# GpSimd pieces beside a two-instruction VectorE step: the wait is set on the instruction ahead of the step

## The chip, the cores and the metric

The kernel runs on one core of a Trainium2 chip. The core has a matrix engine (TensorE, PE in the profile, with its weight loads as PEld), a vector engine (VectorE, DVE), a scalar engine for activation functions (ScalarE, ACT), a general engine (GpSimd, POOL) and a queue engine that issues transfers (SyncE, SP). The engines run their own instruction streams in order and wait for one another on semaphores. The metric is the device time of one execution in microseconds (us); the median of the runs is compared.

## The reference

One transformer block on 2048 rows of 512 numbers, in bfloat16: a layer norm modulated by a vector `c`, self-attention with 32 heads of width 16, a gated residual, a second modulated layer norm, a two-layer network with GELU (512 to 1376 to 512) and a gated residual.

```python
mod = (_silu(c) @ w_mod).reshape(c.shape[0], 6, 1, -1)
sa, ca, ga, sb, cb, gb = (mod[:, i] for i in range(6))
h = _layernorm(x) * (1 + ca) + sa
x = x + ga * attention(h, wqkv, wo)          # 32 heads, Dh = 16, softmax over 2048 keys
h = _layernorm(x) * (1 + cb) + sb
x = x + gb * (gelu(h @ w1 + b1) @ w2 + b2)
```

The attention has 32 x 2048 x 2048 exponentials. They make up most of the work outside the matrix engine.

## The kernel before

The 2048 queries are cut into four blocks of 512. A run is one block with four heads (or, in the last block, half a block with eight), against 16 tiles of 128 keys. TensorE multiplies four heads at a time in four row groups of its array (L864) and writes scores to PSUM. Most scores go to ScalarE, which takes two or three 512-column banks in one exponential (L937, tile `st` to `pt`). The rest go to VectorE, which makes exponentials out of integer arithmetic: an L978 moves 512 scores from PSUM (tile `ax`) to a 16-bit tile `ph`, and when four of them are there, four shifted copies are made. Three or four copies are one VectorE instruction each over all 2048 numbers (L998, the shift, tile `sh`); in many tiles the last copy is made by GpSimd instead, in four pieces of 512 numbers (L1014, tile `sg`). TensorE multiplies all of them with the values (L1049, tile `od`).

Between the runs lies the rest of the block, in small portions: the normalisation of finished heads (GpSimd L1101), the scaling of weights by gates (GpSimd L1124, L1209), and for a finished block its tail. The tail has the output projection and its residual (VectorE L1282), the second layer norm, the two matrix products of the network (TensorE L1238 and L1298, VectorE L1303) and GELU (ScalarE L1308 or L1313). A layer norm takes the statistics of each 128 rows in one VectorE step of two instructions: `bn_stats` (L646, into tile `ln_s`) and `bn_aggr` (L647, into `mv`). GpSimd turns them into a reciprocal root with two small instructions (L651 and L653, tile `rs`), and VectorE applies it (L657, tile `z`).

The order of all instructions is worked out while the program is built, by a planner (class `Plan`). It keeps a clock for every engine, gives each step an estimated cost and a priority, and writes the instructions out in the order in which the steps start on its clocks. Its function `commit` puts one step on its engine and calls the step's function, which emits the instructions. Seeds (`SEEDS`, one for each 16 us) vary the planner's priorities. The engines then run in that fixed order; semaphores alone decide when each instruction starts.

GpSimd pieces are of the kind "beside": the planner places one at the start of a VectorE step that does not use the port which it takes to be shared by the two engines (`port=True` marks the steps that use it: L998 and L657 among those of VectorE). So that the chip keeps to that, each piece gets one added wait by `after_dve`: it looks back through the last 400 instructions emitted, finds the VectorE instructions among them, and waits for the last but one. The last one is taken to be the step beside which the piece is to run. Pieces with this wait are those of L1014, L1101, L1124, L1190, L1209 and L1245.

Of the kernel before, what the change touches and what calls it, by code (L numbers as in the profile page):

```python
# [13 lines left out]
ENG = mybir.EngineType  # L14
# [49 lines left out]
FILL = 2.1  # L64
# [4 lines left out]


class Res:


    def __init__(self, name, n, alloc):
        self.name, self.alloc = name, alloc
        self.free = [0.0] * n
# [34 lines left out]
class Plan:  # L111
    SLACK = {"NIL": 0.0, "PE": 0.10, "DVE": 0.05, "ACT": 0.15, "POOL": 0.05, "SP": 0.05}

    def __init__(self, dyn, later):
        self.later, self.fill_at, self.cool, self.heat, self.until = later, 0.0, 0.0, None, 1e9
        self.free = {e: 0.0 for e in self.SLACK}
        self.lists = {e: [] for e in self.SLACK}
        self.mode, self.tiles, self.now = None, {}, 0.0
        self.bus = {"SP": 0.0, "ACT": 0.0}
        self.port = {"DVE": 0.0, "POOL": 0.0}  # L120
        self.dve = (0.0, 0.0, True)
        self.dyn, self.done, self.fill = dyn, deque(), FILL

    def add(self, op):
        if op.todo == 0:
# [90 lines left out]
    def commit(self, s, o):  # L216
        self.lists[o.eng].remove(o)
        self.now = s
        if o.acq is not None:
            o.slot = min(range(len(o.acq.free)), key=lambda i: o.acq.free[i])  # L220
            o.acq.free[o.slot] = 1e18
            o.tile = o.acq.alloc(o.slot)
        if o.kind == "pv" and s >= self.cool and o.last_left() > 1:
            o.extra, o.us = True, 2 * o.us
        if o.rows is not None:
            o.row = min(o.rows, key=lambda i: self.tiles.get(i, 0.0) if self.mode == "qk" else i)
            o.mode = ("qk", o.row)
        if o.eng == "PE":
            self.done.append((s, (o.us if o.mode[0] != "qk" else o.us * (len(o.mode) - 1) / 4) * o.use))
            while self.done[0][0] < s - 30.0:  # L230
                self.done.popleft()
            tot = 0.0
            self.fill_at = self.cool = 0.0
            for t, us in reversed(self.done):
                tot += us
                if tot >= HEAT and not self.cool:
                    self.cool = t + WIN
                if tot >= self.fill:
                    self.fill_at = t + WIN
                    break  # L240
            if o.mode[0] != self.mode:
                self.mode, self.tiles = o.mode[0], {}
            for i in o.mode[1:]:
                self.tiles[i] = s + o.us
            self.free["PE"] = s + 0.01
        else:
            self.free[o.eng] = s + o.us
            if o.port:
                self.port[o.eng] = s + o.us
            if o.eng == "DVE" and o.us > 0:  # L250
                self.dve = (s, s + o.us, o.port)
        o.end = s + o.us + o.lat
        if o.kb:
            q = "SP"
            self.bus[q] = max(self.bus[q], s + o.us + 0.75) + o.kb / (300.0 if s < 12.0 else 260.0)
            o.end = self.bus[q] + 0.7
        if o.fn is not None:
            o.fn(o)
        for owner in o.rel:
            owner.uses -= 1  # L260
            owner.last = max(getattr(owner, "last", 0.0), o.end + (DVE_PE if o.eng == "DVE" else 0.0))
            if owner.uses == 0:
                owner.acq.free[owner.slot] = owner.last
        for w in o.waiters:
            w.todo -= 1
            w.ready = max(w.ready, o.end + (PV_LATE if o.eng in ("DVE", "POOL", "ACT") and w.kind == "pv" else 0.0))
            if w.todo == 0:
                self.lists[w.eng].append(w)
# [21 lines left out]
def kernel(  # L290
# [14 lines left out]
    nc = tc.nc  # L305
# [115 lines left out]
    plan = Plan(dyn, later)  # L421
# [402 lines left out]
    own = [[kt for kt in range(NT) if kt not in shared[r]] for r in range(NR)]  # L824
# [182 lines left out]
    def by_pool(r, kt, j, first, es, parts):  # L1007
        sh = op("NIL", None, 0.0, es[:1], lat=0.0, prio=0.0, acq=r_sg)
        got = []
        for h in range(4):  # L1010
            def go(o, e=es[h]):
                g_left[0] -= 1
                c = slice(e.qk.row * QB, (e.qk.row + 1) * QB)
                after_dve(nc.gpsimd.tensor_scalar(  # L1014
                    out=sh.tile[:, c], in0=first.tile[:, c], scalar1=1.0 / FINE, scalar2=PH_0 + PH_SH[j],
                    op0=ALU.mult, op1=ALU.add))
            g_left[0] += 1
            got.append(op("POOL", go, G_US, (sh, es[h]), lat=0.1, prio=G_PRIO, kind="beside", rel=(first,), port=True,
                          gate=lambda: plan.beside(G_MIN)))
        pv_op(r, kt, j, got, parts(sh), (sh,))  # L1020
# [111 lines left out]
    def beside(fn, deps, rel=(), prio=0.5, free=False, us=POOL_US):  # L1132

        if free:
            return [op("POOL", lambda o, c=c: fn(slice(c * HB, (c + 1) * HB)), us, deps, lat=0.1, prio=0.1,
                       rel=rel, port=True) for c in range(2)]
        return [op("POOL", lambda o, c=c: after_dve(fn(slice(c * HB, (c + 1) * HB))), us, deps, lat=0.1,
                   prio=prio, kind="beside", rel=rel, port=True, gate=lambda: plan.beside(POOL_MIN))
                for c in range(2)]

    def after_dve(pool):

        own = [i for i in islice(reversed(nc.cur_bb.bb.instructions), 400) if i.engine == ENG.DVE]
        if len(own) > 1:
            tc.add_manual_dep(pool.ins, own[1].name, mybir.DependencyInfo(
                mybir.DependencyClass.Sync, mybir.DependencyReason.DATA), reason="beside")


    o_late = {}

    def late_loads(after):
# [42 lines left out]
    def fold_w1():  # L1194
        sb = op("DVE", lambda o: nc.vector.tensor_copy(out=sb_bf, in_=modB[:, 0:NC]), 0.1, (o_late["mB"],), prio=1.0)

        def column(ps, f):
            for j in range(NC):
                nc.tensor.matmul(out=ps[:, f:f + 1], lhsT=W1[:, j, f * P:(f + 1) * P], rhs=sb_bf[:, j:j + 1],
                                 start=(j == 0), stop=(j == NC - 1))  # L1200
        mm = chain([(lambda ps, f=f: column(ps, f), 0.15) for f in range(NF)], [sb, o_late["w1"]], "gate", r_ax, use=0.05,
                   gate=lambda: plan.cool > plan.now + 0.0)
        o_late["b1"] = op("DVE", lambda o: nc.vector.tensor_tensor(out=b1c, in0=mm.tile[:, 0:NF], in1=b1_bf, op=ALU.add),
                          0.15, (mm, o_late["small"]), prio=1.0, rel=(mm,))
        got = []
        for j in range(NC):
            for lo in range(0, NF * P, QB):
                c = slice(lo, min(lo + QB, NF * P))
                got.append(op("POOL", lambda o, j=j, c=c: after_dve(nc.gpsimd.tensor_scalar(  # L1209
                    out=W1[:, j, c], in0=W1[:, j, c], scalar1=modB[:, NC + j:NC + j + 1], scalar2=0.0,  # L1210
                    op0=ALU.mult, op1=ALU.add)), G_US, (mm, o_late["mB"]), lat=0.1, prio=2.0, kind="beside", port=True,
                    gate=lambda: plan.beside(G_MIN)))
        o_late["w1"] = op("NIL", None, 0.0, got, lat=0.0, prio=0.0)
# [353 lines left out]
```

## Time and profile before

| | |
|---|---|
| median of three runs | 767.43 us (767.27 to 767.84) |
| the profiled execution | 767.62 us |
| its span, first to last instruction | 765.1 us |
| PE busy | 729.2 us, 95% of the span |
| DVE busy | 723.3 us, 95%, 1250 instructions |
| ACT busy | 741.3 us, 97%, 670 instructions |
| POOL busy | 329.3 us, 43%, 603 instructions |
| granted TensorE clock, mean | 0.999 |

A row of a timeline has the start in us from the beginning of the span, the duration in us, the engine, the line in the kernel, the operation, the tile written and the tile read, their shapes, and the count of instructions merged into the row. The bracket at its end is the time for which the engine sat idle before it, and what ended that. A row of a group of instructions has, after the bar, the busy time in us, the mean duration in ns, the idle time before them and who ended it. VectorE rows overlap a little: an instruction is shown to start some 0.08 us before the one ahead has ended. Busy time contains the time in which an instruction that has started is held up.

### The profile page before, as it was taken

To read this page: it belongs to the slowest core of one execution; us is meant where nothing else is said; L and a number is where in the kernel's file an instruction comes from. 1 tells how busy PE (TensorE), PEld (TensorE's weight loads), DVE (VectorE), ACT (ScalarE), POOL (GpSimd) and SP (SyncE) were. 2 spreads that over 40 slices of the span, in tenths; PEclk is the share of its full clock that TensorE was granted. 3 is DMA by queue.
4 is the path that set the end of the run, shared out by engine and by line. 5 is a ranking of instruction groups with operands and counts; after the bars stand their busy time and mean duration, and the time that the engine had idled before them with its cause. 6 is when DMAs were issued, how large, how long until landed. Compare 5 with 4: busy or idle time off the path is not lost. (4 is left out here: it accounts for less than half of the span.)

```text
span 765.1 us, 20651 instructions
## 1 busy us (share of the span) xinstructions
PE 729.2 (95%) x8142; PEld 263.4 (34%) x8142; DVE 723.3 (95%) x1250; ACT 741.3 (97%) x670; POOL 329.3 (43%) x603
## 2 busy tenths in 40 slices
PE   8999999999999999999999999999999899999998
PEld 4423333333322222222322222222233334434454
DVE  7899879999999999999999999999999999999994
ACT  4999999999999999999999999999999999999993
POOL 7513554454444444555455253342434424353421
PEclk9999999999999999999999999999999999999999
DMA  7160010010200001001101010001020102001100
GB/s 221 38 193 26 19 51 18 21 29 12 69 22 25 18 23 47 19 16 40 45 22 42 16 45 18 22 20 33 24 70 22 32 18 60 19 5 46 33 18 28
DMA packets 42162, 29.53 MB, mean 39 GB/s; under 512 B 25525, under 2 KB 35286, under 8 KB 42066
## 3 DMA queue, kind: packets, MB, share of 16 engines
q1 hardware_dynamic: 41530, 27.17, 12.9%
q8 instruction: 63, 1.03, 0.6%
q10 hardware_dynamic: 536, 1.05, 0.4%
q14 instruction: 33, 0.27, 0.1%
HBM read 20.77 MB, written 2.61 MB: 31 GB/s over the span
## 5 line engine op out<-in xcount | busy, mean ns | idle before, releaser
L937 ACT ACTIVATE pt<-st 128x1536 bf16<-128x1536 f32 x618 | 700.8, 1329 | 2.0 <-PE st L864 0.9
L978 DVE TENSOR_SCALAR ph<-ax 128x512 int16<-128x512 f32 x504 | 328.5, 680 | 13.7 <-PE ax L864 12.2
L1014 POOL TENSOR_SCALAR sg<-ph 128x512 int16<-128x512 int16 x316 | 196.4, 622 | 241.9 <-DVE sh L998 168.9
L998 DVE TENSOR_SCALAR sh<-ph 128x2048 int16<-128x2048 int16 x425 | 287.1, 708 | 1.1 <-PE od L1049 0.5
L864 PE MATMUL st<-qm,kT 32*128 32x512 bf16 x1544 | 241.8, 382 | 20.2 <-ACT pt L937 15.4
L864 PE MATMUL ax<-qm,kT 32*128 32x512 bf16 x504 | 174.4, 379 | 4.6 <-DVE ph L978 3.4
L864 PEld LDWEIGHTS <-kT 32*128 32x128 bf16 x2048 | 81.2, 91 | 237.8 <-issue 229.6
L1049 PE MATMUL od<-pt,VEB 128*32 128x512 bf16 (+1 forms) x1924 | 142.6, 341 | 0.2
L1049 PE MATMUL od<-sh,VX 128*32 128x512 bf16 (+1 forms) x1508 | 110.6, 340 | 1.2 <-DVE sh L998 0.6
L1049 PEld LDWEIGHTS <-VEB 128*32 128x32 bf16 x2560 | 61.6, 96 | 80.1 <-issue 65.7
L1049 PEld LDWEIGHTS <-VX 128*32 128x32 bf16 x1908 | 46.0, 95 | 71.7 <-issue 63.0
L1101 POOL TENSOR_TENSOR OT<-OD,RB 128x256 bf16<-128x256 f32 x38 | 28.0, 741 | 59.9 <-DVE sh L998 53.0
L1049 PE MATMUL od<-sh,VEB 128*32 128x512 bf16 (+1 forms) x636 | 49.9, 340 | 0.6 <-DVE sh L998 0.6
L489 PE MATMUL od<-warm 128*32 128x512 bf16 x472 | 45.6, 381 | 0.0
L1298 PE MATMUL ax<-blk,W 128*128 128x512 bf16 (+1 forms) x176 | 43.5, 355 | 0.8 <-DVE ph L978 0.8
L741 PE MATMUL ax<-blk,w 128*128 128x512 bf16 x124 | 35.1, 382 | 1.0 <-DVE ph L978 0.4
L1238 PE MATMUL ax<-w,g 128*128 128x512 bf16 x128 | 34.6, 381 | 1.3 <-DVE ph L978 0.8
L1101 POOL TENSOR_TENSOR OS<-OD,RB 128x256 bf16<-128x256 f32 x24 | 17.3, 728 | 40.8 <-DVE sh L998 30.0
L799 POOL TENSOR_SCALAR VX<-VEB 128x128 bf16<-128x128 bf16 x60 | 20.1, 337 | 31.2 <-DVE VEB L672 27.8
L1049 PE MATMUL od<-sg,VX 128*32 128x512 bf16 (+1 forms) x400 | 32.2, 340 | 0.1
L1303 DVE TENSOR_SCALAR g<-ax,b1c 128x512 bf16<-128x512 f32 (+1 forms) x44 | 29.1, 672 | 0.1
L646 DVE BATCH_NORM_STATS2 ln_s<-xb 128x6 f32<-128x512 bf16 x32 | 21.7, 677 | 1.6 <-DMA xb<-in_A_x_dram 1.4
(107 smaller groups left out, 410.2 us busy)
## 6 DMA issues: line engine op xcount, KB each, us to landing
RB<-rn SPq DMA_DIRECT2D x124, 64.0 KB
xb<-in_A_x_dram SPq DMA_DIRECT2D x7, 512.0 KB
out_dram<-o SPq DMA_DIRECT2D x16, 128.0 KB
qm<-qs SPq DMA_DIRECT2D x120, 16.0 KB
W<-in_B_w_dram SPq DMA_DIRECT2D x1, 1376.0 KB
w<-in_A_wqkv_dram SPq DMA_DIRECT2D x3, 384.0 KB
g<-in_w_mod_dram ACTq DMA_DIRECT2D x1, 1024.0 KB
g<-in_w_mod_dram SPq DMA_DIRECT2D x1, 1024.0 KB
```

What stands on the lines that cost most here:

```text
L489: nc.tensor.matmul(out=o_od[r].tile[32 * i:32 * i + 32, :], lhsT=warm[:, 0:32], rhs=warm[:, 0:1].to_broadcast([P, QB]), start=False, stop= ...
L741: return chain([(lambda ps, j=j: nc.tensor.matmul(out=ps[:, 0:QB], lhsT=w.tile[:, j, cc * P:(cc + 1) * P], rhs=o_h[b].tile[:, j, :], start ...
L864: nc.tensor.matmul(out=o.tile[:, k * QB:(k + 1) * QB], lhsT=kT[cc][kb][rows, ko * P:(ko + 1) * P], rhs=qm.tile[rows, par, :] if hb is None ...
L937: nc.scalar.activation(out=e.tile[:, 0:total * QB], in_=o.tile[:, 0:total * QB], func=ACT.Exp, scale=ESC)
L978: nc.vector.tensor_scalar(out=ph.tile[:, o.row * QB:(o.row + 1) * QB], in0=o.tile, scalar1=PH_B, scalar2=PH_LOW, op0=ALU.add, op1=ALU.max)
L998: nc.vector.tensor_scalar(out=o.tile, in0=first.tile, scalar1=1.0 / FINE, scalar2=PH_0 + PH_SH[j], op0=ALU.mult, op1=ALU.add)
L1014: after_dve(nc.gpsimd.tensor_scalar(out=sh.tile[:, c], in0=first.tile[:, c], scalar1=1.0 / FINE, scalar2=PH_0 + PH_SH[j], op0=ALU.mult, op ...
L1049: nc.tensor.matmul(out=o_od[r].tile[32 * i:32 * i + 32, n * HB:n * HB + w], lhsT=v_tile(kt, ph)[:, c0:c0 + 32], rhs=got[i][:, at:at + w], ...
L1101: two = beside(lambda c: nc.gpsimd.tensor_tensor(out=OT.tile[:, c], in0=OD.tile[:, c], in1=o5.tile[:, c], op=ALU.mult), (OT,), (OD, o5), f ...
L1238: nc.tensor.matmul(out=ps, lhsT=g[:, f, col:col + P], rhs=rhs, start=(f == 0), stop=(f == NF - 1))
L1298: mm = chain([(lambda ps, f=f, j=j, f0=f0: nc.tensor.matmul(out=ps[:, (f - f0) * N:(f - f0 + 1) * N], lhsT=W1[:, j, f * P:(f + 1) * P], rh ...
L1303: ev.append(op("DVE", lambda o, f=f, f0=f0, mm=mm: nc.vector.tensor_scalar(out=g.tile[:, f, 0:N], in0=mm.tile[:, (f - f0) * N:(f - f0 + 1) ...
```

## The change

The added wait is no longer found by counting back from the last VectorE instruction. `commit` calls a new function `mark` just before a VectorE step with a cost emits its instructions, and `mark` notes the VectorE instruction that is then the last. `after_dve` makes the piece wait for the noted one. For a step of one instruction both ways give the same instruction. For the statistics step, L646 and L647, the wait of before is on L646, the step's own first half, and the wait of after is on the instruction ahead of L646. Costs, priorities and seeds are the same.

```diff
-        self.dyn, self.done, self.fill = dyn, deque(), FILL
+        self.dyn, self.done, self.fill, self.mark = dyn, deque(), FILL, None
...
         if o.fn is not None:
+            if o.eng == "DVE" and o.us > 0 and self.mark is not None:
+                self.mark()
             o.fn(o)
...
+    def mark():
+        before[0] = next((i for i in islice(reversed(nc.cur_bb.bb.instructions), 400) if i.engine == ENG.DVE), None)
+
     def after_dve(pool):
-
-        own = [i for i in islice(reversed(nc.cur_bb.bb.instructions), 400) if i.engine == ENG.DVE]
-        if len(own) > 1:
-            tc.add_manual_dep(pool.ins, own[1].name, mybir.DependencyInfo(
+        if before[0] is not None:
+            tc.add_manual_dep(pool.ins, before[0].name, mybir.DependencyInfo(
                 mybir.DependencyClass.Sync, mybir.DependencyReason.DATA), reason="beside")
-
-
+    before, plan.mark = [None], mark
     o_late = {}
```

## The prediction

> **What bounds the kernel now.** I read the page's costliest groups first, for the engine that never rests; then the busy time of the stage in which the edited waits stand; then the chain of waits that ended last. The group of the exponentials:
>
> ```profile
> L937 ACT ACTIVATE pt<-st 128x1536 bf16<-128x1536 f32 x618 | 700.8, 1329 | 2.0 <-PE st L864 0.9
> ```
>
> ScalarE was idle for 2.0 us before all 618 exponentials together. The stage from the first edited place to the end of the exponentials:
>
> ```profile
> 318.00:744.00 426.00, 409.80 (x4816) 144.86 (x4814) 417.22 (x710) 424.72 (x365) 179.08 (x279) 1.00 0.12 31
> ```
>
> The columns are the stretch, its length, and the busy time of PE, weight loads, DVE, ACT and POOL. ACT lacks 426.00 - 424.72 = 1.28 us, DVE 426.00 - 417.22 = 8.78 us, GpSimd is busy for 179.08 us only. So ACT sets the pace, DVE follows close behind, and GpSimd has room. The chain that ended last takes over where the exponentials end:
>
> ```profile
> 743.94 2.65 ACT g L1308 x2
> ```
>
> From there to the end there is no edited wait. What the edit is worth is therefore what ACT gets back before 743.94, and ACT's shown idle time there is 1.28 us.
>
> **What the edit moves.** In the two programs as built, the order of instructions on every engine is the same, and 14 of 608 GpSimd instructions wait for a VectorE count that is lower by one. All 14 stand beside a statistics step of a block's tail, the two instructions L646 and L647. Who waited for the first of them, by the view of the tile `ln_s`:
>
> ```profile
>   POOL sg L1014: 6.1, 9
>   POOL g L1245: 1.2, 1
>   POOL OT L1101: 0.6, 1
>   POOL w L1124: 0.5, 1
>   POOL W2c L1124: 0.5, 1
> ```
>
> That is 13 waits and 8.9 us; the fourteenth found its count reached already, so nothing ended there on L646. No instruction, matmul or transfer is added or removed. A piece may start up to one L646 earlier, 0.69 us in the rows below, unless GpSimd itself is still busy. GpSimd's waiting alone is worth nothing: the engine idles for more than half the stage. It counts only where the late piece gets in the way of VectorE.
>
> **Where it gets in the way.** First place, VectorE, then GpSimd, in order of time:
>
> ```profile
> 319.01 0.68 DVE L978 TENSOR_SCALAR ph<-ax 128x512 int16<-128x512 f32 x1
> 319.60 0.69 DVE L646 BATCH_NORM_STATS2 ln_s<-xb 128x6 f32<-128x512 bf16 x1
> ...
> 320.42 1.17 DVE L998 TENSOR_SCALAR sh<-ph 128x2048 int16<-128x2048 int16 x1
> ```
>
> ```profile
> 318.52 1.32 POOL L1014 TENSOR_SCALAR sg<-ph 128x512 int16<-128x512 int16 x2 [1.24 <-DVE dc L1085]
> 320.37 0.67 POOL L1124 TENSOR_TENSOR w<-w,gb_bc 128x256 bf16<-128x256 bf16 x1 [0.54 <-DVE ln_s L646]
> ```
>
> The piece started 0.08 us after L646 ended (320.29) and ran to 321.04. The shift L998 behind the step began at 320.42, met it, and ended at 321.59, which is 0.55 us after the piece. An unhindered shift takes 0.68 us (613.60 below). So 1.17 - 0.68 = 0.49 us of VectorE was lost. With the edit the piece waits for the L978 ahead, over at 319.69. GpSimd's earlier pair ends at 318.52 + 1.32 = 319.84; with the same 0.08 us the piece runs from 319.92 to 320.59, still 0.17 us into the shift, which then ends at 320.59 + 0.55 = 321.14. VectorE gains **0.45 us**.
>
> Second place, VectorE, GpSimd, TensorE and ScalarE:
>
> ```profile
> 609.85 0.69 DVE L1282 TENSOR_TENSOR xb<-ax,xb 128x512 bf16<-128x512 f32 x1 [0.25 <-PE ax L1232]
> 610.54 0.69 DVE L978 TENSOR_SCALAR ph<-ax 128x512 int16<-128x512 f32 x1
> 611.14 0.68 DVE L646 BATCH_NORM_STATS2 ln_s<-xb 128x6 f32<-128x512 bf16 x1
> ...
> 611.96 1.12 DVE L998 TENSOR_SCALAR sh<-ph 128x2048 int16<-128x2048 int16 x1
> ...
> 613.60 0.68 DVE L998 TENSOR_SCALAR sh<-ph 128x2048 int16<-128x2048 int16 x1
> ```
>
> ```profile
> 608.97 2.01 POOL L1014 TENSOR_SCALAR sg<-ph 128x512 int16<-128x512 int16 x3 [0.55 <-DVE ln_s L646]
> 611.06 0.67 POOL L1124 TENSOR_TENSOR w<-w,ga_bc 128x256 bf16<-128x256 bf16 x1
> 611.92 0.62 POOL L1014 TENSOR_SCALAR sg<-ph 128x512 int16<-128x512 int16 x1 [0.19 <-DVE ln_s L646]
> 612.62 0.53 POOL L651 TENSOR_SCALAR rs<-mv 128x2 f32<-128x2 f32 x1
> 613.23 1.08 POOL L653 TENSOR_TENSOR rs<-rs,mhalf 128x2 f32<-128x2 f32 x1
> ```
>
> ```profile
> 615.74 0.37 PE L864 MATMUL ax<-qm,kT 32*128 32x512 bf16 x1 [0.35 <-DVE ph L978]
> ...
> 616.94 0.40 PE L1049 MATMUL od<-sh,VX 128*32 128x256 bf16 x8 [0.23 <-DVE sh L998]
> ```
>
> ```profile
> 618.41 1.02 ACT L937 ACTIVATE pt<-st 128x1024 bf16<-128x1024 f32 x1 [0.52 <-PE ax L864]
> ```
>
> The shift at 611.96 lost 1.12 - 0.68 = 0.44 us. Two edited waits lie here. The three pieces from 608.97 lost 0.55 us on L646 and may come 0.55 - 0.08 = 0.47 us sooner, so they end at 610.51 instead of 610.98; the `w` behind them may not start before the L1282 that ends at 610.54, so it runs from 610.62 to 611.29; the piece of 611.92 is then released by the L978 that ends at 611.23 and runs from 611.37 to 611.99, out of the shift's way but for 0.03 us. VectorE gains **0.44 us**. If `w` does not move at all, the piece follows its old end (611.73) from 611.81 to 612.43, the shift ends at 612.43 + 0.55 = 612.98, and the gain is 613.08 - 612.98 = 0.10 us. I take 0.44, since every wait in that chain has its release in a row above.
>
> Third place:
>
> ```profile
> 684.46 1.11 DVE L998 TENSOR_SCALAR sh<-ph 128x2048 int16<-128x2048 int16 x1
> ```
>
> ```profile
> 683.28 0.62 POOL L1014 TENSOR_SCALAR sg<-ph 128x512 int16<-128x512 int16 x1
> 684.41 0.62 POOL L1014 TENSOR_SCALAR sg<-ph 128x512 int16<-128x512 int16 x1 [0.51 <-DVE ln_s L646]
> ```
>
> The earlier piece ends at 683.90, so the later one runs from 683.98 to 684.60, the shift ends at 685.15 instead of 685.57, and VectorE gains **0.42 us**.
>
> Fourth place, where it went the other way round:
>
> ```profile
> 447.24 0.68 DVE L978 TENSOR_SCALAR ph<-ax 128x512 int16<-128x512 f32 x1
> ...
> 448.65 0.66 DVE L998 TENSOR_SCALAR sh<-ph 128x2048 int16<-128x2048 int16 x1
> ```
>
> ```profile
> 448.68 1.11 POOL L1014 TENSOR_SCALAR sg<-ph 128x512 int16<-128x512 int16 x1 [1.17 <-DVE ln_s L646]
> ...
> 450.17 0.71 POOL L653 TENSOR_TENSOR rs<-rs,mhalf 128x2 f32<-128x2 f32 x1
> ```
>
> Here the shift came 0.03 us ahead, and the piece lost 1.11 - 0.62 = 0.49 us. Released by the L978 that ends at 447.92, it is over by about 448.7 and may now touch the shift for 0.05 us: VectorE pays **0.05 us**, and GpSimd gains 0.49 us that nobody waits for. The other moved pieces run beside L978, which in the rows keeps its 0.66 to 0.69 us beside a piece; I put them at nothing, with 0.2 us either way each for two or three whose followers shift.
>
> The sum on VectorE is 0.45 + 0.44 + 0.42 - 0.05 = 1.26 us.
>
> **What ACT gets of it.** VectorE had 8.78 us to spare in the stage, so most of its gain turns into VectorE waiting for TensorE. At the second place the way to ACT is in the rows: the matmul at 615.74 waited 0.35 us for an L978, the one at 616.94 0.23 us for a shift, and the exponential at 618.41 came 0.52 us late. Of those 0.52 us the 0.44 come back: **0.44 us**. The other 1.28 - 0.52 = 0.76 us of ACT idle is spread over 426 us; of the gains at the first and third place I count **0.1 us** together, between nothing and 0.76. Sum: 0.5 us, from 0.1 (second place at its low end, nothing elsewhere) to 1.2. The profiled execution took 767.62 us, its span 765.1; the 2.5 us around the span stay. So its span would become 764.6, its time 767.1; against the median of 767.43 the forecast is **766.9 us**.
>
> **Rivals.** *Nothing reaches ACT* (767.3 to 767.6). VectorE's gain ends as VectorE idle, and the late exponential at 618.41 has another cause, since the view names a matmul on `ax`, not VectorE, as its releaser. For it: 8.78 us of VectorE idle. Against it: the two waits of TensorE at 615.74 and 616.94, both on VectorE.
>
> *All of it reaches ACT* (765.9 or less). ACT idle falls by 1.28 us, and small slips of exponentials, which the idle time does not show, fall as well: 767.43 - 1.28 = 766.15, and 0.3 us of slips takes it over the line. Against it: VectorE lies ahead of ACT for most of the stage.
>
> *The small GpSimd pair holds the shift* (767.3). L651 and L653 come earlier too. In the second place the shift now ends at 612.64 and L651 at 612.71, after the 0.07 us it had before. L653 would run from 612.79 to 613.50, if it takes the 0.71 us of the row at 450.17, and the next shift, at 613.60 - 0.44 = 613.16, would start inside it. If the one that starts first keeps the other out, that shift waits 0.34 us and 0.10 of the 0.44 is left: 767.43 - 0.10. Against it: at 613.23 L653 started first, the shift at 613.60 kept its 0.68 us, and L653 stretched to 1.08. [...]
>
> *The statistics themselves are held* (slower, about 770). Thirteen pieces now run beside L646 instead of behind it. If each stretched L646 as the piece at 320.37 stretched the shift, by 0.49 us, VectorE would lose 13 x 0.49 = 6.4 us and, less 1.26, be 5.1 us later; with half of it passed on to ACT the time is 767.43 + 2.6 = 770.0. It decides from 3 us on VectorE, half of which is over 1.5. Against it: the L646 at 611.14 took 0.68 us with the `w` of 611.06 beside it for 0.59 us of its run, and the one at 319.60 took 0.69 with a piece beside it to 319.84.
>
> **How the numbers follow.** Chances: forecast 0.52, nothing reaches ACT 0.26, the pair holds the shift 0.06, all reaches ACT 0.11, statistics held 0.05. About 0.2%, 1.5 us, is what a measurement of this kernel can tell from no change. The first three lie within it, so: faster by more 0.11, within 0.84, slower by more 0.05. The range takes in the forecast's 0.1 to 1.2 us, no gain with the 0.4 us by which the highest run shown lies above the median, and the near part of the full gain: 765.7 to 768.2 us.
>
> **What would show it.** Right: the wait list of `ln_s` holds no GpSimd piece any more; no shift over 1.0 us at the three places; L646 still between 0.63 and 0.70 us; ACT's idle time from 318 to 744 us about 0.8 instead of 1.28 us, and the 0.52 us ahead of 618.41 nearly gone. Wrong: an L646 over 0.8 us, shifts over 0.8 us behind an L653, or ACT idle that stays at 1.28 while the three shifts are short. A time below 765.9 would say that ACT was held by slips that its idle time hides.

## The result and the profile after

The median fell to 765.91 us (765.29 to 766.11, six runs) beside 768.25 us (767.27 to 769.24, six runs) for the kernel before in the same comparison. The ratio is 0.9969 with an interval of [0.9959, 0.998]: faster by 0.31%, more than the 0.2% that the prediction took as the limit of what can be told. The time lies in the stated range, near its low end, but the likeliest case, 0.5 us less, was not what happened; the case that had a chance of 0.11, that all of VectorE's gain reaches ScalarE, was.

The execution profiled after took 765.95 us, its span 764.1. First the page's group of the shifts and that of the exponentials, of the kernel before (the line of its exponentials stands in the prediction) and of the kernel after:

```profile
L998 DVE TENSOR_SCALAR sh<-ph 128x2048 int16<-128x2048 int16 x425 | 287.1, 708 | 1.1 <-PE od L1049 0.5
```

```profile
L937 ACT ACTIVATE pt<-st 128x1536 bf16<-128x1536 f32 x618 | 700.1, 1339 | 1.2 <-PE st L864 0.9
...
L998 DVE TENSOR_SCALAR sh<-ph 128x2048 int16<-128x2048 int16 x425 | 285.8, 705 | 1.2 <-PE od L1049 0.5
```

The shifts cost 287.1 - 285.8 = 1.3 us less; the prediction's sum on VectorE was 1.26. The exponentials lost 2.0 - 1.2 = 0.8 us of idle time, and 700.8 - 700.1 = 0.7 us of **busy** time, though no exponential was changed. Both together are 1.5 us, and that second half is what the forecast had no place for.

The stage, by the windows of the kernel after (stretch, length, busy time of PE, weight loads, DVE, ACT and POOL):

```profile
318.00:743.00 425.00, 403.55 (x4768) 145.55 (x4816) 416.08 (x711) 424.49 (x366) 177.11 (x279) 1.00 0.12 31
```

ACT is idle for 0.51 us where it was idle for 1.28 (up to 744 us); about 0.8 was forecast. Who waited for the tile `ln_s`, after:

```profile
  POOL rs L651: 13.9, 7
  POOL sg L1014: 0.5, 2
```

L651 always waited for it; the two pieces left wait for L647, as the pieces of an ordinary step behind the statistics do. All pieces that waited for L646 are gone from the list.

To compare executions, the document uses one length: from the start of the last cast of keys, in the first 40 us, to the start of the GELU that follows the exponentials in the chain of waits. Nothing edited lies outside it, and the scatter of the first 40 us stays out of it. Timeline of ScalarE, kernel before; then after, with its line from the chain:

```profile
37.64 0.70 ACT L670 CAST kT<-ax 128x512 bf16<-128x512 f32 x1
```

```profile
38.10 0.71 ACT L670 CAST kT<-ax 128x512 bf16<-128x512 f32 x1
```

```profile
742.92 2.65 ACT g L1308 x2
```

Before 743.94 - 37.64 = 706.30 us, after 742.92 - 38.10 = 704.82: the stage is shorter by 1.48 us. Where it goes is seen in ScalarE's timeline at the three places, the same exponentials in both, before and then after:

```profile
319.70 22.34 ACT L937 ACTIVATE pt<-st 128x1536 bf16<-128x1536 f32 x19
...
609.59 8.30 ACT L937 ACTIVATE pt<-st 128x1536 bf16<-128x1536 f32 x7
618.41 4.62 ACT L937 ACTIVATE pt<-st 128x1024 bf16<-128x1024 f32 x4 [0.52 <-PE ax L864]
...
682.75 12.51 ACT L937 ACTIVATE pt<-st 128x1024 bf16<-128x1024 f32 x11
695.43 8.23 ACT L937 ACTIVATE pt<-st 128x1536 bf16<-128x1536 f32 x7 [0.18 <-PE ax L864]
```

```profile
320.19 21.81 ACT L937 ACTIVATE pt<-st 128x1536 bf16<-128x1536 f32 x19
...
609.44 12.99 ACT L937 ACTIVATE pt<-st 128x1536 bf16<-128x1536 f32 x11
...
682.14 20.49 ACT L937 ACTIVATE pt<-st 128x1024 bf16<-128x1024 f32 x18
```

First place: 19 exponentials take 22.34 us, then 21.81, a gain of 0.53, and **no bracket of idle time stands in either row**. Second: 618.41 + 4.62 - 609.59 = 13.44 us, then 12.99, a gain of 0.45, and the bracket of 0.52 is gone. Third: 695.43 + 8.23 - 682.75 = 20.91 us, then 20.49, a gain of 0.42, of which a bracket had shown 0.18. The three make 1.40 of the 1.48 us.

How ScalarE can be late without idle time is seen in single exponentials. Two in a row at the first place, before and then after:

```profile
325.50 1.08 ACT L937 ACTIVATE pt<-st 128x1024 bf16<-128x1024 f32 x1
326.61 1.45 ACT L937 ACTIVATE pt<-st 128x1536 bf16<-128x1536 f32 x1
```

```profile
325.99 1.08 ACT L937 ACTIVATE pt<-st 128x1024 bf16<-128x1024 f32 x1
326.89 1.52 ACT L937 ACTIVATE pt<-st 128x1536 bf16<-128x1536 f32 x1
```

The records of neighbouring exponentials overlap: after, the second starts 326.89 - 325.99 = 0.90 us behind the first, whose record lasts 1.08 us. Before, it starts 1.11 us behind, 0.21 us later, but only the 0.03 us by which it misses the end of the first record count as idle, too little for a bracket. The other 0.18 us took up the overlap that the two records have after (1.08 - 0.90 us).

VectorE at the four places after, in order of time, and then GpSimd:

```profile
320.09 0.68 DVE L646 BATCH_NORM_STATS2 ln_s<-xb 128x6 f32<-128x512 bf16 x1
...
320.91 0.71 DVE L998 TENSOR_SCALAR sh<-ph 128x2048 int16<-128x2048 int16 x1
...
448.55 0.66 DVE L998 TENSOR_SCALAR sh<-ph 128x2048 int16<-128x2048 int16 x1
...
610.99 0.68 DVE L646 BATCH_NORM_STATS2 ln_s<-xb 128x6 f32<-128x512 bf16 x1
...
611.81 0.66 DVE L998 TENSOR_SCALAR sh<-ph 128x2048 int16<-128x2048 int16 x1
...
612.99 0.68 DVE L998 TENSOR_SCALAR sh<-ph 128x2048 int16<-128x2048 int16 x1
...
683.86 0.69 DVE L998 TENSOR_SCALAR sh<-ph 128x2048 int16<-128x2048 int16 x1
```

```profile
320.40 0.67 POOL L1124 TENSOR_TENSOR w<-w,gb_bc 128x256 bf16<-128x256 bf16 x1
...
447.97 0.62 POOL L1014 TENSOR_SCALAR sg<-ph 128x512 int16<-128x512 int16 x1 [0.57 <-DVE ph L978]
...
610.47 0.67 POOL L1124 TENSOR_TENSOR w<-w,ga_bc 128x256 bf16<-128x256 bf16 x1
611.22 0.62 POOL L1014 TENSOR_SCALAR sg<-ph 128x512 int16<-128x512 int16 x1
...
612.63 1.08 POOL L653 TENSOR_TENSOR rs<-rs,mhalf 128x2 f32<-128x2 f32 x1
```

The three long shifts of 1.17, 1.12 and 1.11 us now take 0.71, 0.66 and 0.69: 0.46, 0.46 and 0.42 less, where 0.45, 0.44 and 0.42 were worked out. The L646 at 610.99 keeps its 0.68 us with pieces beside it for 0.60 us of its run.

### The profile page after: what moved, and what is told of

The parts are those of the page before. It is cut to its first block, busy times and chain, and to the rows that moved or that the text cites. A ratio compares the mean times of both kernels' runs of the same rounds, so it can differ in the third digit from the quotient of the medians.

```text
span 764.1 us, 20575 instructions
## 1 busy us (share of the span) xinstructions
PE 719.9 (94%) x8067; PEld 264.0 (35%) x8142; DVE 721.8 (94%) x1250; ACT 740.6 (97%) x670; POOL 327.2 (43%) x603
## 5 line engine op out<-in xcount | busy, mean ns | idle before, releaser
L937 ACT ACTIVATE pt<-st 128x1536 bf16<-128x1536 f32 x618 | 700.1, 1339 | 1.2 <-PE st L864 0.9
L978 DVE TENSOR_SCALAR ph<-ax 128x512 int16<-128x512 f32 x504 | 328.9, 681 | 13.8 <-PE ax L864 12.0
L998 DVE TENSOR_SCALAR sh<-ph 128x2048 int16<-128x2048 int16 x425 | 285.8, 705 | 1.2 <-PE od L1049 0.5
L864 PE MATMUL st<-qm,kT 32*128 32x512 bf16 x1544 | 241.8, 383 | 24.1 <-ACT pt L937 17.7
L864 PE MATMUL ax<-qm,kT 32*128 32x512 bf16 x504 | 174.8, 379 | 4.3 <-DVE ph L978 3.1
L864 PEld LDWEIGHTS <-kT 32*128 32x128 bf16 x2048 | 82.1, 91 | 239.6 <-issue 231.4
L1298 PE MATMUL ax<-blk,W 128*128 128x512 bf16 (+1 forms) x155 | 41.0, 352 | 1.8 <-DVE ph L978 0.6
L1238 PE MATMUL ax<-w,g 128*128 128x512 bf16 x116 | 32.7, 382 | 2.1 <-DVE ph L978 0.8
L741 PE MATMUL ax<-blk,w 128*128 128x512 bf16 x99 | 32.1, 382 | 2.6 <-issue 0.8
L646 DVE BATCH_NORM_STATS2 ln_s<-xb 128x6 f32<-128x512 bf16 x32 | 21.7, 678 | 1.9 <-DMA xb<-in_A_x_dram 1.7
```

What stands on the lines that cost most here:

```text
L741: return chain([(lambda ps, j=j: nc.tensor.matmul(out=ps[:, 0:QB], lhsT=w.tile[:, j, cc * P:(cc + 1) * P], rhs=o_h[b].tile[:, j, :], start ...
L864: nc.tensor.matmul(out=o.tile[:, k * QB:(k + 1) * QB], lhsT=kT[cc][kb][rows, ko * P:(ko + 1) * P], rhs=qm.tile[rows, par, :] if hb is None ...
L937: nc.scalar.activation(out=e.tile[:, 0:total * QB], in_=o.tile[:, 0:total * QB], func=ACT.Exp, scale=ESC)
L978: nc.vector.tensor_scalar(out=ph.tile[:, o.row * QB:(o.row + 1) * QB], in0=o.tile, scalar1=PH_B, scalar2=PH_LOW, op0=ALU.add, op1=ALU.max)
L998: nc.vector.tensor_scalar(out=o.tile, in0=first.tile, scalar1=1.0 / FINE, scalar2=PH_0 + PH_SH[j], op0=ALU.mult, op1=ALU.add)
L1238: nc.tensor.matmul(out=ps, lhsT=g[:, f, col:col + P], rhs=rhs, start=(f == 0), stop=(f == NF - 1))
```

## The experiments

The theory (A in the expectations): VectorE's lateness is passed on to ScalarE in full, through TensorE, whose matmul on `ax` at 615.74 waited 0.35 us for an L978 with the kernel before, and most of that never shows as idle time of ScalarE. The rivals: the gain comes from the ten moved pieces that met no shift; from GpSimd being earlier, whatever VectorE does; or only the one late exponential at 618.41 came back and the rest is scatter. Other letters stand for the rivals of that one expectation.

The planner breaks ties by a hash of a step's first line number. The change, and every kernel below, keep the line numbers, so that the order of the instructions is the same in all.

All runs in one table. The ratio is to the kernel before, run on the same chip in the same batch (medians 767.48, 767.64 and 768.38 us for the three batches). "Stage" is the length defined above.

| run | median us (lowest to highest, runs) | ratio [95%] | stage us |
|---|---|---|---|
| before, after (first profiles) | 768.25, 765.91 | 0.9969 [0.9959, 0.998] | 706.30, 704.82 |
| edit_again | 765.5 (765.29 to 766.8, 10) | 0.9974 [0.9962, 0.9986] | 704.89 |
| four_pieces | 766.09 (765.39 to 768.82, 12) | 0.998 [0.9966, 0.9993] | 705.45 |
| ten_pieces | 767.14 (766.55 to 768.57, 12) | 0.9988 [0.9978, 0.9999] | 705.83 |
| first_place | 767.3 (766.4 to 770.38, 12) | 0.9994 [0.9981, 1.0007] | 705.97 |
| one_later | 768.23 (767.49 to 770.19, 10) | 1.0009 [0.9999, 1.002] | 706.83 |
| dose_tight | 768.49 (767.95 to 769.74, 10) | 1.0006 [0.9996, 1.0016] | 707.09 |
| dose_slack | 767.22 (766.42 to 769.35, 10) | 0.9998 [0.9986, 1.0009] | 707.10 |
| last_port | 766.0 (765.28 to 766.34, 7) | 0.9971 [0.996, 0.9982] | 705.09 |
| edit_third | 766.12 (765.46 to 768.16, 11) | 0.9973 [0.9964, 0.9983] | 704.83 |
| same_before | 767.76 (767.28 to 770.08, 11) | 0.9998 [0.9989, 1.0008] | 706.66 |

**Is the size real?** Two repeats of the change, and the kernel before against itself, none with a further edit.

> The change as a whole, timed in pairs against the kernel before. Theory A (every stall that VectorE loses reaches ScalarE in full): 1.5 us faster than the kernel before, ratio 0.9980, as the shift of the exponentials between the two profiles says (0.48 us later at 10 us, 1.02 us earlier at 695 us). Rival B (the forecast: only what ScalarE's shown idle time covers comes back): 0.5 us faster, 0.9993. Rival C (something beside the moved waits helps, as the medians of the first comparison suggest): 2.3 us faster, 0.9970.

> The change again, for the rate of runs in which the granted TensorE clock falls below 0.999 (so far 0 of 16 with the change, 10 of 62 before it), and for the difference in runs without that. Theory A: 1.4 to 1.7 us between the medians of runs at full clock. If the change also makes the clock drops rarer: at most 1 of 10 again. If their rate is the same: 1 or 2 of 10, and about 2 us longer each.

> The kernel before against itself: ratio 1.0000, and its interval says how far two samples of one kernel lie apart here. 1 or 2 of 10 runs below 0.999 of the clock if the rate so far holds.

In three comparisons the change gave 0.9969, 0.9974 and 0.9973, and the kernel before against itself 0.9998 with 1 inside its interval. In the profiles the stage takes 706.30 and 706.66 us before, and 704.82, 704.89 and 704.83 with the change: 1.4 to 1.8 us less. The gain is no scatter. The medians differ by some 2.0 to 2.3 us, more than the stage does. What is left over, 0.1 to 0.9 us, no run here settles; two samples of the kernel before in the last batch, with medians of 768.38 and 767.76 us, differ by 0.62 us themselves.

**Which of the 14 pieces?** Three kernels move the wait for a part of the pieces alone; in order of emission, the 1st piece stands at the first place, the 11th and 12th at the second and the 14th at the third. `four_pieces` moves these four, `ten_pieces` the other ten (the one of the fourth place among them), `first_place` the 1st alone.

```diff
     def after_dve(pool):
-        if before[0] is not None:
-            tc.add_manual_dep(pool.ins, before[0].name, ...
+        own = [i for i in islice(reversed(nc.cur_bb.bb.instructions), 400) if i.engine == ENG.DVE]
+        if len(own) > 1:
+            n_two[0] += own[1].name != before[0].name
+            to = before[0] if own[1].name != before[0].name and n_two[0] in (1, 11, 12, 14) else own[1]
+            tc.add_manual_dep(pool.ins, to.name, ...
```

Here `own[1]` is the instruction for which the kernel before waits. In `ten_pieces` the set is `(2, 3, 4, 5, 6, 7, 8, 9, 10, 13)`, in `first_place` it is `(1,)`.

> Only 4 of the 14 waits are moved: the pieces at 320, 609, 612 and 684 us, whose shifts VectorE had to wait with. Theory A: VectorE gains 0.45 + 0.47 + 0.41 = 1.3 us and the time falls by 1.3 us (1.1 to 1.5), nearly all of the change's gain. Rival B: 0.5 us. Rival D (the gain is spread over all moved waits, 14 equal parts): 0.4 us.

> The other 10 of the 14 waits are moved, the 4 of the collisions with a shift stay as before. Theory A: 0.1 to 0.3 us faster, since these pieces stand beside instructions that they do not hold up. Rival D: 10/14 of the gain, 1.0 us or more. The GpSimd instructions end earlier here too, by 0.3 to 1.5 us in each place, so if early GpSimd work were what counts it would show here.

> One wait alone is moved, the piece at 320 us. ScalarE shows no idle time of over 0.1 us there. Theory A: VectorE gains 0.45 us and all exponentials from about 340 us on come 0.45 us earlier than with the kernel before, the time falls by 0.4 to 0.5 us. Rival B: exponentials behind it move by 0.1 us or less, the time is the same.

Nineteen exponentials from the first place on, in ScalarE's timeline of `first_place` and `ten_pieces`:

```profile
320.25 21.88 ACT L937 ACTIVATE pt<-st 128x1536 bf16<-128x1536 f32 x19
```

```profile
320.26 22.19 ACT L937 ACTIVATE pt<-st 128x1536 bf16<-128x1536 f32 x19
...
618.48 5.54 ACT L937 ACTIVATE pt<-st 128x1024 bf16<-128x1024 f32 x5 [0.52 <-PE ax L864]
```

The first piece alone brings the place from 22.34 to 21.88 us, 0.46 of the change's 0.53; the ten others bring 0.15 there, and leave the late exponential of the second place at its 0.52 us. The three long shifts keep their 1.17, 1.12 and 1.11 us in `ten_pieces`, and are down to 0.71, 0.66 and 0.69 us in `four_pieces`. The stage of `ten_pieces` is 0.47 us shorter than that of before: besides the 0.15 us, 0.26 us are at 408 us, where the change itself gains nothing and a transfer varies (below), and the small rest is spread. Two profiles of the kernel before differ by 0.36 us in the stage themselves. So in the profiles the collisions at the three places carry most of the gain, and the ten others a few tenths at most. The clock says less: the ratio of `ten_pieces` is 0.9988, about 0.9 us with anything from 0.1 to 1.7 us in its interval, and that interval overlaps with the one of `four_pieces`. `first_place` is worth too little for the clock to resolve: its ratio holds 1. `four_pieces` has 0.998 where the change has 0.9974, and its interval holds both; its stage is 0.56 us longer than that of `edit_again`. Of these, 0.34 us is one stall of ScalarE that the change's runs don't have at this place, here in the timeline of VectorE of `four_pieces`:

```profile
404.80 0.25 DVE L1085 RECIPROCAL dc<-dc 128x16 f32<-128x16 f32 x1 [0.64 <-DMA dc<-dn]
```

VectorE waited 0.64 us for a transfer, and 3.5 us later, at 408.34, an exponential is 0.34 us late. In the other profiles that wait was between 0.51 us (`last_port`) and none that is shown (`ten_pieces`, `dose_tight`). Whether the 0.64 us is chance or comes of the pieces left where they were, this run does not say.

**Earlier GpSimd, or an unhindered VectorE?** `one_later` makes the 1st, 12th and 14th piece wait for L647: one instruction later than before, so that GpSimd loses time, but at the first place the piece can no longer start ahead of the shift. All other pieces wait as in the kernel before. The edit against that of `four_pieces`:

```diff
-            to = before[0] if own[1].name != before[0].name and n_two[0] in (1, 11, 12, 14) else own[1]
+            to = own[0] if own[1].name != before[0].name and n_two[0] in (1, 12, 14) else own[1]
```

> The kernel before, with three waits moved the other way: the pieces at 320, 612 and 684 us wait for L647, one instruction later than before, so that the shift comes first and the piece is the one held up. Theory A with the chain of the small pair (VectorE's own waiting counts wherever it comes from): at 320 us VectorE gains 0.4 to 0.5 us although GpSimd is later; at 612 and 684 us the piece ends later, L651 and L653 behind it too, and the L657 that needs them comes 0.3 to 0.4 us later than before; in all 0.2 to 0.3 us slower than the kernel before. Rival F (only the shift's own stretch counts): VectorE gains 0.45 us at each place, 1.3 us faster. Rival G (GpSimd must be early everywhere): slower at all three places.

Timelines of `one_later`, VectorE, GpSimd and ScalarE:

```profile
320.92 0.66 DVE L998 TENSOR_SCALAR sh<-ph 128x2048 int16<-128x2048 int16 x1
...
614.93 0.74 DVE L657 TENSOR_SCALAR z<-xb,mv,rs 128x512 bf16<-128x512 bf16 x2 [0.90 <-POOL rs L653]
```

```profile
321.08 1.65 POOL L1124 TENSOR_TENSOR w<-w,gb_bc 128x256 bf16<-128x256 bf16 x2 [0.75 <-DVE mv L647]
...
612.34 0.97 POOL L1014 TENSOR_SCALAR sg<-ph 128x512 int16<-128x512 int16 x1 [0.40 <-DVE mv L647]
```

```profile
320.20 21.84 ACT L937 ACTIVATE pt<-st 128x1536 bf16<-128x1536 f32 x19
```

At the first place GpSimd's piece starts 0.68 us later than with the change (321.08 against 320.40), the shift is short all the same, and the 19 exponentials take 21.84 us: the gain is there with a **later** GpSimd. That the piece itself had to come earlier falls, for this place. At the other two places the shift went first too, but now the late piece took 0.97 us, pushed L651 and L653 back, and VectorE waited 0.90 us for them at each of the two, ahead of an L657 that shows no such wait with the kernel before. ScalarE lost there (the stage is 0.53 us longer than the profile of before, with the first place won), and the kernel came out no faster than before, 1.0009. So what counts in these rows is when VectorE goes on, by whichever cause.

**Does VectorE's lateness always reach ScalarE?** Two kernels add one or more VectorE instructions of 0.69 us to the change, a `bn_stats` of a finished tile whose result nobody reads, behind an L1074 that is there already: `dose_tight` in runs 8, 9 and 10, where VectorE shows no idle time behind it, `dose_slack` in runs 21 and 29, where it shows some.

```diff
-        OD = op("DVE", lambda o: nc.vector.tensor_copy(out=o.tile, in_=od.tile), 0.6, (last,),
+        OD = op("DVE", lambda o: (nc.vector.tensor_copy(out=o.tile, in_=od.tile), r in (8, 9, 10) and nc.vector.bn_stats(out=work.tile([P, 6], FP32, name="ex", bufs=1), in_=o.tile)), 0.6, (last,),
```

> The changed kernel with one more VectorE instruction behind three of the copies L1074, at about 226, 247 and 270 us: a bn_stats of 0.6 us start to start that nobody reads. VectorE shows no idle time of over 0.1 us from 196 to 300 us. Theory A (in a stretch without VectorE idle each loss passes to ScalarE): the exponentials behind come 0.5 to 0.6 us later after each, 1.6 to 1.8 us in all, and the time grows by 1.5 to 1.8 us. Rival B (ScalarE sets the pace and VectorE has slack): 0 to 0.5 us.

> The changed kernel with the same extra VectorE instruction behind two copies L1074 that have VectorE idle time soon behind them: at 514 us (idle 0.53 us at 526 and 0.30 at 531) and at 703 us (0.73 us at 708 and 0.76 at 717). Theory A with slack counted by place: the idle times take the delay up, the exponentials move by 0.3 us or less in all. Rival H (every VectorE loss passes on, wherever it is): 1.1 to 1.2 us later.

The first dose in VectorE's timeline of `dose_tight`:

```profile
226.69 0.69 DVE L1074 BATCH_NORM_STATS2 ex<-OD 128x6 f32<-128x512 f32 x1
```

The exponentials over the three doses in ScalarE's timeline of `dose_tight`:

```profile
232.36 21.02 ACT L937 ACTIVATE pt<-st 128x1536 bf16<-128x1536 f32 x18 [0.19 <-PE st L864]
253.55 22.01 ACT L937 ACTIVATE pt<-st 128x1536 bf16<-128x1536 f32 x19 [0.17 <-PE ax L864]
275.98 16.05 ACT L937 ACTIVATE pt<-st 128x1024 bf16<-128x1024 f32 x14 [0.41 <-PE st L864]
```

And the window around them, `dose_tight` and then the change without them (`edit_again`); the fourth of the five busy times is ScalarE's:

```profile
200.00:320.00 120.00, 112.13 (x1197) 34.29 (x1197) 119.88 (x198) 118.94 (x106) 54.05 (x84) 1.00 0.09 24
```

```profile
200.00:320.00 120.00, 113.47 (x1212) 35.26 (x1205) 119.74 (x199) 120.00 (x107) 55.29 (x87) 1.00 0.09 23
```

The stage of `dose_tight` is 707.09 - 704.89 = 2.20 us longer for three instructions of 0.69 us (2.07 us together), so each is passed on whole. But ScalarE's brackets show 0.19 + 0.17 + 0.41 = 0.77 us, and with the gaps too short for a bracket it is idle for 120.00 - 118.94 = 1.06 us, where the change without doses has none. This is the plainest measure of the case: here the cause is known, its size is known, and half of it doesn't appear as idle time of the engine that sets the pace. By which matmul the lateness reaches ScalarE is in the rows only where a bracket names one (L864, tile `st` or `ax`); at the first place, without a bracket, that path is argued and not shown.

`dose_slack` speaks against one part of the theory. I had held that a dose costs nothing where VectorE is seen idle soon after. The stage grew by 707.10 - 704.89 = 2.21 us for two doses. A part of that belongs, by my estimate, to the granted clock of TensorE, which was 0.52 for 3.5 us in this execution; two exponentials behind it came 0.80 and 0.39 us late (below). But the median of its ten runs, seven of them with a granted clock of 1.0 in the mean, is 767.22 us, 1.2 us over `last_port` on the same chip, which ties with the change: of 2 x 0.69 = 1.38 us most is paid in any case. The second dose, at 704.62 us, shows it by itself, at a granted clock of 1.00. The timelines of VectorE and ScalarE in `dose_slack`, then of VectorE in `edit_again`:

```profile
710.38 0.69 DVE L1326 TENSOR_TENSOR o<-ax,xb 128x512 bf16<-128x512 f32 x1 [0.66 <-PE ax L1238]
```

```profile
707.53 15.11 ACT L937 ACTIVATE pt<-st 128x1536 bf16<-128x1536 f32 x13 [0.48 <-PE st L864]
```

```profile
707.99 0.69 DVE L1326 TENSOR_TENSOR o<-ax,xb 128x512 bf16<-128x512 f32 x1 [0.65 <-PE ax L1238]
```

Ahead of the dose VectorE's copy L1074 starts 1.78 us later than in `edit_again` (703.90 against 702.12), behind it L1326 2.39 us later. ScalarE shows 0.48 us of idle time there, and in `edit_again` none. VectorE's wait for TensorE ahead of L1326 is the same in both: it moved along with the delay instead of taking it up. So idle time of VectorE in this trace is no slack by itself.

**Would more of the same bring more?** `last_port` goes further: a piece waits for the last VectorE step that the planner marks `port=True`, and steps in between no longer hold it back. 224 of 608 waits come earlier than with the change, or fall away. In the trace of the kernel before, the two kinds so marked, L998 and L657, take 0.68 and 0.41 us in the median and up to 1.17 and 0.87, while none of the 504 L978 and 32 L646 takes over 0.70. That a port is what the two engines share is the planner's assumption; no run shows it.

```diff
-                self.mark()
+                self.mark(o.port)
...
-    def mark():
-        before[0] = <the last VectorE instruction>
+    def mark(port):
+        before[0], was[0] = <the last VectorE instruction> if was[0] else before[0], port
```

> A version meant to beat the change: each GpSimd piece waits for the last VectorE shift (L998) or L657 ahead of its step, not for whatever instruction is ahead, since only these collide with GpSimd in the traces; 224 of 608 waits come earlier or go. Theory A: shifts that are now stretched by 0.1 to 0.3 us by the end of a piece (some 80 of 425) are freed in part, VectorE gains 2 to 6 us, and 1 to 4 us of that reach ScalarE: 761.5 to 764.5 us. Rival I (the chain of pieces on GpSimd or the data they read sets their start, not this wait): same as the change, 765.5 us.

In angle brackets stands the search of the last 400 instructions, shortened. The shifts on the pages of `last_port` and of the change (`edit_again`):

```profile
L998 DVE TENSOR_SCALAR sh<-ph 128x2048 int16<-128x2048 int16 x425 | 284.0, 700 | 1.3 <-PE od L1049 0.5
```

```profile
L998 DVE TENSOR_SCALAR sh<-ph 128x2048 int16<-128x2048 int16 x425 | 286.2, 706 | 1.2 <-PE od L1049 0.5
```

VectorE's shifts lost another 2.2 us of hindrance, and the time did not follow: 0.9971 beside 0.9974 and 0.9973, a stage of 705.09 beside 704.89. The 1 to 4 us expected did not come. From 200 us on its exponentials start 0.16 to 0.35 us later than those of `edit_again`, 0.22 us at 200 us and 0.28 us at the end, so none of them gains or loses more than 0.2 us on the way. The collisions that this removes had cost ScalarE nothing that the profiles show. A loss on VectorE was passed on in both dose kernels (2.20 us of the stage for 2.07 us, 1.2 us of the median for 1.38); a gain seems to count only where that delay had reached ScalarE already, which fits all runs here but was not tried by itself. `last_port` does not beat the change.

## Why the prediction was right or wrong

**What bounds the kernel: right.** ScalarE sets the pace up to its GELU at 743.94 us, and the gain came before it.

**What the edit moves: right.** The statistics released no piece afterwards.

**The three collisions: right to 0.02 us.** 0.45, 0.44 and 0.42 us were worked out from the ends of pieces; the shifts lost 0.46, 0.46 and 0.42. At the second place the lower end, 0.10, was not needed: the chain from the three pieces over `w` to the last piece moved as its releases allowed (611.22 to 611.84 us, out of the shift's way). At the fourth place the shift kept its 0.66 us where 0.05 was to be paid; by the prediction's own rows the piece would end at 447.92 + 0.08 + 0.62 = 448.62 us, ahead of the shift at 448.65, so that this price did not follow from them. The other moved pieces, put at nothing, brought 0.15 us at the first place in `ten_pieces` and a few tenths in all by the profiles, and did no harm; the clock alone would allow more.

**What ACT gets of it: the step that failed.** "Of the gains at the first and third place I count 0.1 us together, between nothing and 0.76". They brought 0.53 and 0.42. The 0.44 of the second place were right (0.45). The mistake was the bound: the 0.76 us of idle time left to ScalarE were taken as all that could be got back there. Behind it stood two readings, and both fell. *ScalarE's idle time is not its lateness*: the exponentials of the first place are shorter by 0.53 us with no bracket before or after, and `dose_tight` shows 1.06 of 2.20 us. The records of exponentials overlap, so that a wait of 0.21 us at 326.61 showed as 0.03 us idle, and the group's busy time fell by 0.7 us with the work unchanged. And *VectorE's 8.78 us to spare are not slack*: `dose_slack` paid for its doses, with VectorE's idle time behind the second still there, 0.66 us beside 0.65.

**The rivals.** *All of it reaches ACT* is what happened, and for the reason that the prediction gave beside it, slips of exponentials which the idle time does not show. Its price, 767.43 - 1.28 - 0.3, was 765.9 or less; the median was 765.91. The parts were not as priced: 0.8 of the 1.28 us of idle time came back, and 0.7 us instead of 0.3 in slips, so that the agreement of the sum is luck. The chance of 0.11 was too low, since the argument against it, VectorE lying ahead, came from the same misread idle time. *Nothing reaches ACT* fell with the second place's bracket. *The small pair holds the shift* fell: L653 started first, at 612.63, and the shift of 612.99 kept its 0.68 us, while L653 took 1.08. No run shows the 0.34 us by which the shift would have been held. With the kernel before, the shifts that started behind a piece of 128x256 or 128x512 at the three places were held, to 1.17, 1.12 and 1.11 us; the one at 613.60, behind this instruction of 128x2, kept its 0.68. *The statistics held* fell: L646 took 0.68 us beside pieces from 610.47 and 611.22.

Had the three gains been passed on in full, the forecast's own sum would have been 767.43 - 1.26 = 766.2 us, near the 765.9 measured. The forecast of 766.9 us was 1.0 us too high; the time lies in the range because the range had been drawn to take in the near part of the full gain, not because the sum on ScalarE was right.

## What to carry to other kernels

Where an engine's records can cover its waits, its idle time gives a floor for what it loses, not a ceiling (in `dose_tight` 1.06 of 2.20 us): take one stretch of the same instructions from first start to last end, and see whether it is as short as elsewhere. Price a collision on a feeding engine at full worth until a run with a known dose says otherwise, and don't call that engine's idle time slack before asking whose lateness it is waiting for. More collisions removed is not more gain: 1.3 us of them at three places brought 1.4 us and more, another 2.2 us brought nothing.

## What the runs showed of the hardware

**In the profiled `dose_slack` TensorE's granted clock was 0.52 for 3.5 us, behind 3.5 us in which it was idle for 1.27.** Windows of `dose_slack` around its first dose, of the change (`edit_again`), and of a stretch of `four_pieces`; the number behind the five busy times, of which TensorE's is the first, is the granted clock:

```profile
513.00:516.50 3.50, 2.23 (x18) 0.69 (x14) 3.46 (x6) 3.49 (x2) 1.70 (x4) 1.00 0.01 2
516.50:520.00 3.50, 3.50 (x31) 0.64 (x23) 2.92 (x6) 3.47 (x3) 1.07 (x3) 0.52 0.07 12
```

```profile
513.00:516.50 3.50, 2.86 (x23) 0.81 (x22) 3.50 (x7) 3.49 (x2) 1.85 (x3) 1.00 0.03 7
```

```profile
403.00:406.50 3.50, 2.02 (x12) 0.72 (x11) 2.82 (x7) 3.47 (x3) 1.80 (x4) 1.00 0.11 19
406.50:410.00 3.50, 3.50 (x29) 1.17 (x28) 3.47 (x8) 3.16 (x4) 3.04 (x5) 1.00 0.34 78
```

And behind the drop ScalarE's timeline in `dose_slack`:

```profile
523.15 1.02 ACT L937 ACTIVATE pt<-st 128x1024 bf16<-128x1024 f32 x1 [0.80 <-PE ax L864]
```

With the dose TensorE was busy for 2.23 of 3.50 us, 64%, and then had a granted clock of 0.52 for 3.5 us; without it, 2.86 of 3.50 us, the clock stayed at 1.00. Two exponentials came 0.80 and 0.39 us late in the microseconds that followed. The share alone doesn't explain the drop: in `four_pieces` TensorE was busy for less, 2.02 of 3.50 us, and kept its clock of 1.00. Nor does the dose alone: the mean clock was below 0.999 in three of its ten runs only. What decides stays open.

**The first microseconds scatter by more than the change is worth.** The profiled execution of `edit_third` took 768.16 us with a stage as short as the others: its GELU starts at 745.13 us, that of `edit_again` at 742.37, behind stages of 704.83 and 704.89 us. Its first window:

```profile
0.00:20.00 20.00, 16.52 (x114) 7.33 (x114) 12.88 (x33) 7.72 (x11) 12.44 (x49) 0.91 0.68 211
```

The granted clock was 0.91 in the mean there, 300 us ahead of the first edited instruction. Of 94 runs of the kernel before in the three batches 13 had a granted clock below 0.999, of 27 runs of the change 2; that the change alters this rate is not shown.
